# Threshold attention and an exact-GELU MLP on one core: the first batch's x^T by halves, identity matmuls in two kinds of slots, and an MLP share dealt over two slots

## The chip, the cores and the metric

The kernel runs on one core of one Trainium2 chip. The metric is the device time of one launch in microseconds. Two changes in time can be told apart here when they differ by about 0.3%, some 4 us.

## The reference

All of it is float32. q, k and v are (batch 8, heads 8, sequence 576, head dimension 64), tau is a scalar of 0.02. Attention keeps the scores near the maximum of each row:

```
scores = q k^T / sqrt(64)
thresh = rowmax(scores) - tau
scores = where(scores >= thresh, scores, -1e9)
attn   = exp(scores - rowmax);  attn /= sum(attn) + 1e-9
x      = attn v                       # (8, 8, 576, 64)
x      = x transposed to (4608, 512)  # heads side by side
h      = x w_in                       # w_in 512 x 2048
y      = gelu_exact(h) w_out          # w_out 2048 x 512
```

The output y is (4608, 512).

## The kernel before

**Pairs, chunks and slots.** Two heads of one batch are a pair: 32 pairs, of which the first batch has numbers 0 to 3. A pair's 576 query rows are five chunks: four of 128 rows for each head, and one of 64 rows with both heads together. The main loop goes over slots n, one for each pair p and chunk i, in this order: chunks 0 and 1 of pairs 0 to 3 (n = 0 to 7), chunks 2 to 4 of pairs 0 to 3 (n = 8 to 19), and from BATCH = 20 on the five chunks of pair 4, of pair 5, and so on. The weights and the later inputs are still being loaded while the first batch runs.

**A slot.** Everything is written out by hand, in the order in which the engines shall take it; each engine works through its own list in that order.

1. `scores` (L403): TensorE multiplies the chunk with k, two heads at a time, into two PSUM buffers with the tag "sc"; there are two of them, so the next slot's scores wait until this slot has done with its own.
2. `softmax_head`: VectorE takes the row maxima (L415), ScalarE the exponentials (L418), GpSimd the thresholds (L416). Between the thresholds GpSimd adds the low bits of a piece of weights (L226).
3. In the first batch, what is `due`: `weigh_v` multiplies the weights of the pair's finished rows with v to x^T (L538) into a PSUM buffer with the tag "mm", and ScalarE copies it to its place in the token block (L548); `divide_early` spreads the reciprocal sums by matmuls (L457), ScalarE copies them (L459), and GpSimd multiplies x^T by them (L465).
4. `fill` gives TensorE a share of the MLP: matmuls of the first layer (L614) or of the second (L629). How many is a matter of a planner's debt: `owed` is the planned progress in blocks of 256 tokens times the planner's price of a block, and each matmul takes its planner's price off it.
5. `turn_p_early` of the slot before: TensorE transposes the weights (L349) into "mm" buffers and ScalarE copies them to pT (L356, L365), where x^T needs them.
6. `softmax_tail`: VectorE keeps the weights that reach the threshold and sums them (L435); in the first batch the sums go to a small tile with the tag "den", of which there are four.
7. `convert`: ScalarE (L202, L203) and VectorE (L210, L212) turn pieces of w_in and w_out, which came in as raw bits, into float32; GpSimd's addition follows in a later slot.

From slot 20 on `fill` stands at the end of a slot, `turn_p` is a VectorE transpose (L499), and the regrouping is done by DMA.

**Where the first batch's x^T stands.** Rows 0 to 255 of a pair are chunks 0 and 1. Chunk 1 of pair p is computed in slot 2p + 1, turned in the next slot, and put on `due` at the end of that one; so x^T of those 256 rows is made in slot 2p + 3. Slots 4, 6 and 8 come between and have no x^T; of these, slots 6 and 8 have scores and transposes alone (slot 4 has the turning of pair 3's q and k beside them). Rows 256 to 575 follow in the same manner after chunk 4. The first MLP matmul needs the first 256 rows of all four pairs, and is planned for slot 10.

**PSUM.** The tag "mm" has four buffers, which go round in turn: x^T, divisors, transposes and both MLP layers allocate from it.

**Slot 20.** It is the first of the second batch; the held GELUs of the first token block are run there, so `fill` is left out and what is owed goes to slot 21.

**Start.** Before the loop VectorE zeroes `q_tail` and all of the four v tiles (L1028), since parts of a v tile's last chunk stay unwritten.

Of the kernel before, what the change touches and what calls it, by code (L numbers as in the profile page):

```python
# [8 lines left out]
FP32 = mybir.dt.float32  # L9
# [9 lines left out]
def kernel(  # L19
# [28 lines left out]
    nc = tc.nc  # L48
    ctx.enter_context(tc.manual_schedule())

    B, H, S, D = q.shape
    d_model, d_ff = moe_w_in.shape
    P = 128
    Q = 32
    HP = H // 2
    NP = B * HP
    EARLY = HP
    NC = S // P
# [4 lines left out]
    KR = -(-NB // 4)  # L63
    N_DM = d_model // P
    N_DF = d_ff // P
    TOK = 256
# [6 lines left out]
    SLOTS = NC + 1  # L73
# [4 lines left out]
    small = ctx.enter_context(tc.tile_pool(name="small", bufs=4))  # L78
    dram = ctx.enter_context(tc.tile_pool(name="dram", bufs=1, space=bass.MemoryType.DRAM))
    ps = ctx.enter_context(tc.tile_pool(name="ps", bufs=4, space=PSUM))  # L80
# [4 lines left out]
    xall = const.tile([P, XSLOTS, N_DM, TOK], FP32, name="xall")  # L85
# [14 lines left out]
    x_at = {}  # L100

    def x_slot(want=None):
        i = max(x_free) if want is None else want
        x_free.remove(i)
        return i

    def x_place(n):

        last = XSLOTS - 1
        if n >= PLAIN + len(AWAY):  # L110
            return min(x_free)
        return last if n == PLAIN - 1 else max(i for i in x_free if i < last or n < 3)
# [8 lines left out]
    ident = const.tile([P, P], FP32, name="ident")  # L121
# [3 lines left out]
    q_tail = [att.tile([P, P], FP32, name=f"q_tail{i}") for i in range(4)]  # L125
    v_sb = [att.tile([P, 2, KR, D], FP32, name=f"v{i}") for i in range(4)]
# [18 lines left out]
    idle = ps.tile([P, 2 * P], FP32, tag="mm", name="idle")  # L145
# [98 lines left out]
    st = {}  # L244
    x_blk = {}
# [48 lines left out]
    def load_v_early(p):  # L294
        b, hp = divmod(p, HP)
        t = st[p]["v"] = v_sb[p % 4]
        for e in range(2):
            nc.sync.dma_start(t[:, e, 0:NC, :], v[b, 2 * hp + e, 0:MAIN, :].rearrange("(p t) d -> p t d", p=P))
            nc.sync.dma_start(t[e * TAIL:(e + 1) * TAIL, e, NC, :], v[b, 2 * hp + e, MAIN:S, :])

    def turn_qk_early(p):


        s = st[p]
        if 2 <= p < HP:
            qT = op.tile([P, MAIN], FP32, tag="o_sb", name="qT")
            kT = pd_tail[p - 2].rearrange("p b i -> p (b i)")
        else:
            qT = ld.tile([P, MAIN], FP32, tag="qT", name="qT")
            kT = ld.tile([P, TAIL + S], FP32, tag="kT", name="kT")  # L310
        s["qT"], s["kT"] = qT, kT
        qt = s["q_tail"] = q_tail[p % 4]
        copy = nc.scalar.copy if p else nc.vector.tensor_copy
        for name in "qk":
            t = s[name]
            tr = ps.tile([P, NC, P], FP32, tag="mm", name="tr")
            for c in range(NC):
                for e in range(2):
                    nc.tensor.matmul(tr[e * D:(e + 1) * D, c, :], lhsT=t[:, e, c, :], rhs=ident, start=True, stop=True)
            src = tr.rearrange("p c s -> p (c s)")  # L320
            if name == "q":
                nc.scalar.activation(qT, src, AF.Copy, bias=0.0, scale=q_scale)
            else:
                copy(kT[:, TAIL:S], src)
        tr = ps.tile([P, NC, P], FP32, tag="mm", name="tr")
        for j, name in enumerate("qk"):
            t = s.pop(name)
            for e in range(2):
                nc.tensor.matmul(tr[e * D:(e + 1) * D, j, 0:TAIL], lhsT=t[0:TAIL, e, NC, :],
                                 rhs=ident[0:TAIL, 0:TAIL], start=True, stop=True)  # L330
        x_free.extend(s.pop(name + "_slot") for name in "qk" if name + "_slot" in s)
        nc.scalar.copy(kT[:, S:S + TAIL], tr[:, 1, 0:TAIL])
        nc.scalar.copy(kT[D:P, 0:TAIL], tr[D:P, 1, 0:TAIL])
        for e in range(2):
            rows = slice(e * D, (e + 1) * D)
            nc.scalar.activation(
                qt[rows, e * TAIL:(e + 1) * TAIL], tr[rows, 0, 0:TAIL], AF.Copy, bias=0.0, scale=q_scale[rows])
# [84 lines left out]
    def softmax_tail(p, i):  # L422

        s = st[p]
        sc, thr, w = s.pop(("sc", i)), s.pop(("thr", i)), s["p", i]
        n = len(sc)
        if p < EARLY:
            pair = small.tile([P, 2], FP32, tag="den", name="den")
            den = [pair[:, e:e + 1] for e in range(n)]
        else:  # L430
            at = [e * NC + i if i < NC else 2 * NC for e in range(n)]
            den = [sums[p % 2][:, x:x + 1] for x in at]
        for e in range(n):
            row = w[:, e * S:(e + 1) * S].rearrange("p (h s) -> p h s", h=2)
            nc.vector.scalar_tensor_tensor(  # L435
                row, sc[e][:, :, 0:HALF], thr[:, e:e + 1], row, op0=ALU.is_ge, op1=ALU.mult, accum_out=den[e])
        if p < EARLY:
            nc.gpsimd.tensor_scalar(pair[:, 0:n], pair[:, 0:n], 1e-9, None, op0=ALU.add)
            s["sum", i] = pair[:, 0:n]
# [6 lines left out]
    def divide_early(p, lo, hi):  # L446


        s = st[p]
        b, hp = divmod(p, HP)  # L450
        tr = ps.tile([P, 512], FP32, tag="mm", name="tr")
        for i in range(lo // P, -(-hi // P)):
            den = s.pop(("sum", i))
            to = tr[:, i * P - lo:min((i + 1) * P, hi) - lo]
            for e in range(2):
                one_of, cols = (den[:, e:e + 1], ident) if i < NC else (den, ident[:, e * TAIL:(e + 1) * TAIL])
                nc.tensor.matmul(to[e * D:(e + 1) * D, :], lhsT=one_of.to_broadcast([P, D]), rhs=cols, start=True, stop=True)  # L457
        by = dg.tile([P, S], FP32, tag="inv", name="inv")
        nc.scalar.copy(by[:, 0:hi - lo], tr[:, 0:hi - lo])  # L459
        for n, o, at, size in in_blocks(b, lo, hi):  # L460
            x, y = x_blk[n][:, hp, o:o + size], by[:, at - lo:at - lo + size]
            if size == TOK:
                x = x.rearrange("q (p c) -> q c p", c=2)
                y = y.rearrange("q (c p) -> q c p", c=2)
            nc.gpsimd.tensor_tensor(x, x, y, op=ALU.mult)  # L465
# [57 lines left out]
    def weigh_v(p, lo, hi):  # L523


        b, hp = divmod(p, HP)
        s = st[p]
        xT = ps.tile([P, 512], FP32, tag="mm", name="xT")
        for c in range(KR):
            for e in range(2):  # L530
                f = slice(e * D, (e + 1) * D)
                to = xT[f, 0:hi - lo]
                if p < EARLY:
                    rhs = s["pT"][0 if c == NC else e][:, c, lo:hi]
                else:
                    to = to.rearrange("p (g s) -> p g s", s=2 * Q)
                    rhs = by_64(s["pT"][e])[:, lo // (2 * Q):hi // (2 * Q), c, :]
                nc.tensor.matmul(  # L538
                    to, lhsT=s["v"][:, e, c, :], rhs=rhs, start=(c == 0), stop=(c == KR - 1))
        for n, o, at, size in in_blocks(b, lo, hi):  # L540
            if n not in x_blk:
                x_at[n] = x_slot(x_place(n))
                x_blk[n] = xall[:, x_at[n], :, :]
            to, x = x_blk[n][:, hp, o:o + size], xT[:, at - lo:at - lo + size]
            if p < EARLY and size == TOK:
                to = to.rearrange("q (p c) -> q c p", c=2)
                x = x.rearrange("q (c p) -> q c p", c=2)
            nc.scalar.copy(to, x)  # L548

    def in_blocks(b, lo, hi):  # L550
        while lo < hi:
# [86 lines left out]
    def fill(ns, tokens):  # L638

        mlp["debt"] += ns  # L640
        while True:
            if mlp["next"] is None:
                n = mlp["n"]
                if n == PLAIN or (n + 1) * TOK > tokens:
                    break
                mlp["steps"] = block_steps(n)
                mlp["n"] += 1
                mlp["next"] = next(mlp["steps"])
            took, need = mlp["next"]
            if mlp["debt"] <= 0 or need > converted[0]:  # L650
                break
            mlp["debt"] -= took
            mlp["next"] = next(mlp["steps"], None)
# [370 lines left out]
    for _ in range(2):  # L1024
        load_piece(nc.gpsimd)
    load_early(2)
    for t in q_tail + v_sb:
        nc.vector.memset(t, 0.0)  # L1028
    turn_qk_early(0)
    conv["steps"] = conversions()  # L1030
# [10 lines left out]
    BATCH = HP * SLOTS  # L1041
# [15 lines left out]

    PARTS = 1.3, 1.3, 0.2, 1.3, 0.9

    tokens = 0  # L1060
    owed = 0.0
    due = []
    leaving = []
    loads = iter(())
    for n in range(len(slots) + WEIGH + 1):
# [16 lines left out]
            gelus_held()  # L1082
        table()
        for args in due:
            weigh_v(*args)
            divide_early(*args)
        due = []
# [47 lines left out]
        if not early:  # L1135
            lag[0] = 2 if p < NP else 0
            if n != BATCH:
                fill(owed, tokens)
                owed = 0.0
        if last and last[0] < EARLY:  # L1140
            if last[1] == 1:
                due.append((last[0], 0, TOK))
            if last[1] == NC:
                due.append((last[0], TOK, S))
# [44 lines left out]
```

## Time and profile before

| | |
|---|---|
| median of three runs | 1352.2 us (1350.23 to 1354.08) |
| profiled span | 1351.2 us |
| TensorE busy | 1326.1 us (98%) |
| VectorE busy | 1043.9 us (77%) |
| ScalarE busy | 605.6 us (45%) |
| GpSimd busy | 657.2 us (49%) |
| mean granted TensorE clock | 0.989 |
| first batch (slots 0 to 19), by the scores' starts | 9.4 to 134.4 us |

TensorE (PE in the profile, PEld for its weight loads) is busy nearly all the time, but busy time is also time at a low clock: the profile gives the clock that was granted in each stretch beside it. VectorE is DVE, ScalarE is ACT, GpSimd is POOL. L12 is line 12 of the kernel. A group of instructions is told by its line, engine, operation and tiles. A matmul in fp32 stands in the trace as two instructions, a transpose as one.

### The profile page before, as it was taken

To read this page: it belongs to the slowest core of one execution; us is meant where nothing else is said; L and a number is where in the kernel's file an instruction comes from. 1 tells how busy PE (TensorE), PEld (TensorE's weight loads), DVE (VectorE), ACT (ScalarE), POOL (GpSimd) and SP (SyncE) were. 2 spreads that over 40 slices of the span, in tenths; PEclk is the share of its full clock that TensorE was granted. 3 is DMA by queue.
4 is the path that set the end of the run, shared out by engine and by line. 5 is a ranking of instruction groups with operands and counts; after the bars stand their busy time and mean duration, and the time that the engine had idled before them with its cause. 6 is when DMAs were issued, how large, how long until landed. Compare 5 with 4: busy or idle time off the path is not lost.

```text
span 1351.2 us, 19824 instructions
## 1 busy us (share of the span) xinstructions
PE 1326.1 (98%) x6282; PEld 895.3 (66%) x6282; DVE 1043.9 (77%) x2005; ACT 605.6 (45%) x1027; POOL 657.2 (49%) x1091
## 2 busy tenths in 40 slices
PE   8899899999999999999999999999999999999998
PEld 6577457467467467457557557568787787877877
DVE  6877687788888888878888888874758698385775
ACT  7877437438447538437638536413201112211120
POOL 4766444555655565554554551144363513635530
PEclk8899899999999999999999999999999999999999
DMA  8743276677778687787688677500000031000003
GB/s 258 188 137 76 67 168 147 149 169 182 159 179 176 159 202 168 162 207 167 153 210 181 150 180 150 117 8 0 1 0 1 16 110 32 0 1 0 1 0 78
DMA packets 209782, 152.40 MB, mean 113 GB/s; under 512 B 113360, under 2 KB 193088, under 8 KB 209680
## 3 DMA queue, kind: packets, MB, share of 16 engines
q1 hardware_dynamic: 187648, 110.43, 37.1%
q0 software_dynamic: 21312, 39.37, 10.5%
q10 hardware_dynamic: 720, 1.34, 0.3%
q8 instruction: 51, 0.84, 0.3%
q14 instruction: 51, 0.42, 0.1%
HBM read 55.97 MB, written 12.52 MB: 51 GB/s over the span
## 4 chain that ended last, share of the span: by engine, by line
PE 93%; ACT 2%; DMA 2%; DVE 1%; issue 1%; POOL 0%; SPq 0%; DVEq 0%; ACTq 0%; POOLq 0%
PE bank L802 34%; PE o_ps L629 17%; PE hT L614 16%; PE sc L403 14%; PE xT L538 11%; DMA x<-xall 1%; DMA q<-in_q_dram 1%; ACT p L418 1%; PE tr L349 1%; DVE nmx L415 1%; ACT pT L356 0%; DVE p L435 0%; PE tr L457 0%; ACT power L202 0%; DVE power L212 0%
## 5 line engine op out<-in xcount | busy, mean ns | idle before, releaser
L418 ACT ACTIVATE p<-sc,nmx 128x576 f32<-128x576 f32 x288 | 201.9, 739 | 278.7 <-DVE nmx L415 278.5
L435 DVE SCALAR_TENSOR_TENSOR p<-sc,thr,p 128x576 f32<-128x576 f32 x288 | 226.2, 816 | 77.9 <-ACT p L418 71.4
L416 POOL TENSOR_SCALAR thr<-nmx,tau_eff 128x1 f32<-128x1 f32 x288 | 85.3, 296 | 369.0 <-DVE nmx L415 359.4
L415 DVE TENSOR_REDUCE nmx<-sc 128x1 f32<-128x576 f32 x288 | 205.4, 750 | 53.4 <-PE sc L403 52.1
L614 PE MATMUL hT<-xall,w_in 128*128 128x256 f32 x1024 | 243.0, 387 | 0.0
L629 PE MATMUL o_ps<-w_out,g 128*128 128x512 f32 x512 | 238.4, 606 | 0.0
L614 PEld LDWEIGHTS hT<-xall,w_in 128*128 128x128 f32 x1024 | 190.4, 191 | 50.5 <-issue 23.0
L684 DVE TENSOR_TENSOR c<-c,bank 128x320 f32<-128x320 f32 x304 | 147.2, 488 | 33.7 <-PE bank L802 20.5
L684 DVE TENSOR_TENSOR o<-o,bank 128x256 f32<-128x256 f32 x240 | 99.8, 420 | 93.7 <-PE bank L802 88.7
L403 PE MATMUL sc<-kT,qT 64*128 64x288 f32 x960 | 161.8, 434 | 9.8 <-DVE p L435 9.1
L538 PE MATMUL xT<-pT,v 128*64 128x256 f32 (+1 forms) x1280 | 168.0, 416 | 0.1
L629 PEld LDWEIGHTS o_ps<-w_out,g 128*128 128x128 f32 x512 | 93.7, 191 | 110.2 <-issue 107.6
L499 DVE STREAM_TRANSPOSE turned_p<-p 128x1152 f32<-128x1152 f32 x112 | 154.4, 1378 | 3.9
L403 PEld LDWEIGHTS sc<-kT,qT 64*128 64x128 f32 x960 | 92.2, 188 | 83.4 <-issue 69.5
L538 PEld LDWEIGHTS xT<-pT,v 128*64 128x64 f32 x1280 | 91.4, 140 | 75.3 <-issue 14.6
L802 PE MATMUL bank<-w_out,c 128*128 128x256 f32 x480 | 120.2, 381 | 0.5 <-DVE o L684 0.5
L269 POOL DMA_DIRECT2D v<-in_v_dram x208 | 111.3, 538 | 3.7 <-issue 1.3
L802 PEld LDWEIGHTS bank<-w_out,c 128*128 128x128 f32 x480 | 89.9, 190 | 18.8 <-DVE o L684 3.0
L855 ACT ACTIVATE c<-c 128x320 f32<-128x320 f32 (+1 forms) x80 | 46.9, 623 | 114.6 <-DVE c L684 114.5
L684 POOL TENSOR_TENSOR c<-c,g 128x320 f32<-128x320 f32 (+1 forms) x40 | 50.6, 1273 | 67.4 <-DVE c L684 67.4
L802 PE MATMUL bank<-t_out,c 128*128 128x256 f32 x320 | 82.7, 381 | 0.0
L802 PE MATMUL bank<-t_out,g 128*128 128x256 f32 x320 | 82.1, 379 | 0.0
(179 smaller groups left out, 1771.8 us busy)
## 6 DMA issues: line engine op xcount, KB each, us to landing
pT<-turned_p SPq DMA_DIRECT2D x448, 160.0 KB, 3.6
pT<-pd_tail SPq DMA_DIRECT2D x112, 80.0 KB, 3.0
q<-in_q_dram POOLq DMA_DIRECT2D x104, 72.0 KB, 3.8
k<-in_k_dram POOLq DMA_DIRECT2D x104, 72.0 KB, 3.2
inv<-turned SPq DMA_DIRECT2D x54, 128.0 KB, 4.0
v<-in_v_dram POOLq DMA_DIRECT2D x156, 40.0 KB, 3.1
out_dram<-o SPq DMA_DIRECT2D x40, 128.0 KB, 2.4
xall<-in_moe_w_out_dram POOLq DMA_DIRECT2D x9, 512.0 KB, 4.4
```

The costliest lines, as they stand in the source:

```text
L269: eng.dma_start(t[r:P:4, e, 0:n, :], rows[:, r * KR:r * KR + n, :])
L403: nc.tensor.matmul(sc[e][:, h, 0:HALF], lhsT=lhsT, rhs=s["kT"][rows, at:at + HALF], start=True, stop=True)
L415: nc.vector.tensor_reduce(nmx[:, e:e + 1], sc, axis=AXIS.XY, op=ALU.max, negate=True)
L416: nc.gpsimd.tensor_scalar(thr[:, e:e + 1], nmx[:, e:e + 1], -1.0, tau_eff, op0=ALU.mult, op1=ALU.subtract)
L418: nc.scalar.activation(w[:, e * S:(e + 1) * S].rearrange("p (h s) -> p h s", h=2), sc, AF.Exp, bias=nmx[:, e:e + 1], scale=1.0)
L435: nc.vector.scalar_tensor_tensor(row, sc[e][:, :, 0:HALF], thr[:, e:e + 1], row, op0=ALU.is_ge, op1=ALU.mult, accum_out=den[e])
L499: nc.vector.transpose(turned_p[:, :, i // 2, 0:NB, i % 2 * Q:(i % 2 + 1) * Q], w.rearrange("p (e b i) -> p e b i", e=2, i=Q))
L538: nc.tensor.matmul(to, lhsT=s["v"][:, e, c, :], rhs=rhs, start=(c == 0), stop=(c == KR - 1))
L614: nc.tensor.matmul(hT[:, j % 2, :], lhsT=w_in_sb[c][:, j * P:(j + 1) * P], rhs=x_blk[n][:, c, :], start=(c == 0), stop=(c == N_DM - 1))
L629: nc.tensor.matmul(o[:, 0:d_model], lhsT=g[j][:, m * P:(m + 1) * P], rhs=w_out_sb[j], start=(j == 0), stop=(j == N_DF - 1))
L684: eng.tensor_tensor(out, a, b, op=ALU.add)
L802: nc.tensor.matmul(to, lhsT=l, rhs=r, start=start and k == 0, stop=k == len(pairs) - 1, skip_group_check=not start)
```

## The change

All of it concerns the first batch and the two slots after it.

- `weigh_half` makes x^T of one chunk, 128 rows, of pairs 2 and 3 as soon as that chunk is turned: chunk 0 in slots 6 and 8, chunk 1 (with the division of both) in slots 7 and 9.
- `keep_busy` multiplies the identity with itself into an "mm" buffer that nobody reads: four fp32 matmuls at the end of slots 6 and 8, eight at the end of slot 20. It is there to hold TensorE's clock up where it would otherwise have nothing to do.
- What is owed to the MLP at slot 21 is dealt out as 0.4 of it in slot 21, and the rest in slot 22.
- The tag "den" has ten buffers instead of four.
- Of the v tiles only the last chunk is zeroed at the start.

```diff
+    def keep_busy(times):
+        idle = ps.tile([P, 2 * P], FP32, tag="mm", name="idle")
+        for _ in range(times):
+            for c in range(2):
+                nc.tensor.matmul(idle[:, c * P:(c + 1) * P], lhsT=ident, rhs=ident, start=True, stop=True)
...
-            pair = small.tile([P, 2], FP32, tag="den", name="den")
+            pair = small.tile([P, 2], FP32, tag="den", name="den", bufs=2 * SLOTS)
...
+    def weigh_half(p, c):
+        hp = p % HP
+        s = st[p]
+        if 0 not in x_blk:
+            x_at[0] = x_slot(x_place(0))
+            x_blk[0] = xall[:, x_at[0], :, :]
+        xT = ps.tile([P, 512], FP32, tag="mm", name="xT")
+        cols = slice(c * P, (c + 1) * P)
+        for k in range(KR):
+            for e in range(2):
+                nc.tensor.matmul(xT[e * D:(e + 1) * D, 0:P], lhsT=s["v"][:, e, k, :],
+                                 rhs=s["pT"][0 if k == NC else e][:, k, cols], start=(k == 0), stop=(k == KR - 1))
+        nc.scalar.copy(x_blk[0][:, hp, :].rearrange("q (p c) -> q c p", c=2)[:, c, :], xT[:, 0:P])
...
-    for t in q_tail + v_sb:
+    for t in q_tail + [t[:, :, NC, :] for t in v_sb]:
         nc.vector.memset(t, 0.0)
...
+    HALVED = (2, 3)
+    BUSY = {6: 2, 8: 2, BATCH: 4}
...
         for args in due:
+            if len(args) == 2:
+                weigh_half(*args)
+                if args[1]:
+                    divide_early(args[0], 0, TOK)
+                continue
             weigh_v(*args)
             divide_early(*args)
...
             if n != BATCH:
-                fill(owed, tokens)
-                owed = 0.0
+                share = 0.4 if n == BATCH + 1 else 1.0
+                fill(owed * share, tokens)
+                owed *= 1.0 - share
+        if n in BUSY:
+            keep_busy(BUSY[n])
         if last and last[0] < EARLY:
-            if last[1] == 1:
+            if last[1] < 2 and last[0] in HALVED:
+                due.append((last[0], last[1]))
+            elif last[1] == 1:
                 due.append((last[0], 0, TOK))
```

## The prediction

> **What bounds the kernel now.** I read the page's 40 slices first: where is TensorE not busy, and where is its clock below full?
>
> ```profile
> PE   8899899999999999999999999999999999999998
> ...
> PEclk8899899999999999999999999999999999999999
> ```
>
> Only slices 0, 1 and 4 (33.8 us each) have a clock digit of 8. Busy time by stage (columns: us of the stage, busy us and instructions of PE, PEld, DVE, ACT and POOL, granted clock, DMA share, GB/s) says the same:
>
> ```profile
> 10.00:170.00 160.00, 145.21 (x870) 98.32 (x869) 117.49 (x236) 115.04 (x229) 97.84 (x161) 0.92 0.51 141
> 165.00:1351.20 1186.20, 1178.80 (x5379) 793.65 (x5378) 925.11 (x1759) 488.62 (x793) 558.37 (x925) 1.00 0.48 108
> ```
>
> After 165 us TensorE is busy 99.4% at clock 1.00: nothing in the change shortens that, and whatever time is won before it should move the end one for one, since its fills, loads and softmaxes are written out in a fixed order. Before it 14.8 us are idle and the clock is 0.92.
>
> Next the TensorE timeline of the first batch, for gaps. A bracket gives the idle time before and its releaser; "xN" are instructions, and an fp32 matmul is two of them.
>
> ```profile
> 43.44 1.20 PE L349 MATMUL tr<-ident,p 128*128 128x128 f32 x9
> 47.41 3.42 PE L403 MATMUL sc<-pd_tail,qT 64*128 64x288 f32 x8 [2.77 <-DVE p L435]
> 50.77 4.06 PE L538 MATMUL xT<-pT,v 128*64 128x256 f32 x20
> ...
> 61.14 3.01 PE L403 MATMUL sc<-kT,qT 64*128 64x288 f32 x8 [2.44 <-DVE p L435]
> 64.08 4.23 PE L538 MATMUL xT<-pT,v 128*64 128x256 f32 x20
> ...
> 138.24 0.72 PE L403 MATMUL sc<-kT,qT 64*128 64x288 f32 x2 [1.94 <-DVE p L435]
> ...
> 158.20 1.94 PE L403 MATMUL sc<-kT,qT 64*128 64x288 f32 x8 [1.58 <-DVE p L435]
> 160.07 6.21 PE L629 MATMUL o_ps<-w_out,g 128*128 128x512 f32 x10
> ```
>
> These are slots 7, 9, 21 and 23. Each gap is in a slot with scores and transposes alone, and after each the same instructions run long: eight score matmuls take 1.24 us elsewhere (at 42.27), the twenty of x^T 2.65 (at 37.91), ten of the second layer 4.56 (at 171.03). Cut into stretches of 3.41 us the clock is seen to switch whole stretches:
>
> ```profile
> 43.76:47.18 3.42, 0.88 (x9) 0.64 (x6) 3.24 (x6) 3.24 (x6) 1.96 (x3) 1.00 0.83 226
> 47.18:50.59 3.41, 3.18 (x8) 1.70 (x8) 3.00 (x8) 3.19 (x7) 2.75 (x6) 0.53 0.25 96
> 50.59:54.00 3.41, 3.41 (x17) 1.91 (x18) 2.93 (x7) 1.41 (x2) 2.57 (x5) 0.50 0.90 252
> ...
> 57.41:60.83 3.42, 1.29 (x11) 0.97 (x9) 2.50 (x5) 3.42 (x7) 2.68 (x5) 1.00 0.72 256
> 60.83:64.24 3.41, 3.10 (x10) 1.97 (x12) 3.38 (x9) 3.23 (x7) 2.75 (x4) 0.53 0.13 50
> ...
> 77.89:81.30 3.41, 2.46 (x14) 1.67 (x14) 2.93 (x8) 3.19 (x8) 3.06 (x4) 1.00 0.18 73
> ...
> 135.92:139.33 3.41, 1.09 (x6) 0.43 (x4) 2.92 (x8) 2.89 (x4) 2.77 (x4) 1.00 0.00 0
> 139.33:142.74 3.41, 3.37 (x12) 1.82 (x14) 3.33 (x7) 3.40 (x7) 1.02 (x7) 0.53 0.02 5
> ...
> 156.40:159.81 3.41, 1.81 (x9) 1.00 (x8) 3.16 (x6) 1.39 (x2) 2.67 (x6) 1.00 0.42 94
> 159.81:163.22 3.41, 3.41 (x6) 1.50 (x5) 3.37 (x7) 0.56 (x1) 0.91 (x2) 0.53 0.27 65
> ```
>
> A stretch with 0.88, 1.29, 1.09 or 1.81 us of matmuls is followed by one at half clock; one with 2.46 is not. So the line lies somewhere between 53% and 72% busy.
>
> **What the skill says.** "TensorE: Matmul & The Clock Gate", Part 1, says that the clock is either half or full and is judged over a free-running window of 3413 ns; the stretches above agree (0.50 to 0.53 or 1.00, edges a multiple of 3.41 us apart). Its "HAM oscillation" section asks for no idle gap above some 3.4 us; the trace is stricter: a gap of 1.58 us sufficed, and the trace decides. The section on the array's architecture says that ScalarE and VectorE are strict FIFOs; the trace agrees (the copy of x^T at 54.90 stands behind both exponentials of its slot), and it matters below.
>
> **The change, part by part.** First site, slots 6 to 9. The gap before 47.41 ends with VectorE's threshold product of slot 6, so filling it does not shorten slot 6; it may keep the clock up in slot 7. There the work was 3.42 + 4.06 + 0.44 (divisors) + 1.13 (transposes), about 8.9 us. With half of x^T gone to slot 6 and full clock it is 1.17 + 1.45 + 0.45 + 1.13 = 4.2. Halves cost what wholes do: twenty instructions of 64 weight columns by 128 at 70 ns, taken between the 66 ns of L319 (16 in about 1.05 us) and the 75 ns of L457 (8 in 0.60): 1.4 us, against 2.65 for 256 columns. Two halves are thus dearer by 0.15 us, in slack.
>
> TensorE then no longer sets slots 7 to 9; ScalarE does. Its chain, copied from the trace: it starts slot 6's conversions at 48.00. A new copy of a half x^T (0.28, as the 128-column L365) stands before, so 48.3. Exponentials of slot 7 follow at 51.87 (before 51.59), 1.41; half x^T 0.28; divisors 0.37; pT copies up to the next conversion 1.25: 55.2, against 57.06 (it sat idle 1.91 before 54.90 for x^T). Slot 8: conversions 2.25, exponentials 1.24, the second new copy 0.28, pT 1.1: 60.1, against 61.66. Slot 9: VectorE's maxima are held by these conversions, so the exponentials start at 63.2 (64.77 less 1.6), then 1.41, 0.28, 0.37, 1.25: 66.5, against 70.54. Slot 10's scores may start when slot 9's first product frees their bank, 66.61 - 1.6 = 65.0, and end at 66.0. But the first MLP matmul needs pair 3's division on GpSimd, which stands behind two weight additions: 67.98 - 1.6 + 0.8 = 67.2. So L614 starts at 67.3 instead of 70.85: **3.5 us**. From there to slot 20 TensorE has only seven gaps with 2.7 us in all, so this is carried.
>
> The identity matmuls: slots 6 and 8 get 4 (8 instructions), slot 20 gets 8 (16). The trace has no 128x128 fp32 matmul with 128 weight columns; L349's transposes run at 107 to 126 ns (9 in 1.13), the L614 rate halved gives 108, and at half clock it would be double. I take 120: 0.95 us and 1.9 us; the ends are 0.85 and 1.9 for the former. They add a wait: the "mm" buffers go round four at a time (at 35.84 the second transposed group waits for qT's copy, four allocations back). In slots 6 and 8 the allocations are x^T, three for transposes, then idle: so idle waits for the copy of x^T, which stands behind the exponentials, to 47.3 and 59.0. Queued behind it are the next scores, free at 47.6 and about 59.4: they start at 48.3 and 60.0, 0.6 to 0.7 late. Who waits for the scores is VectorE's maxima, which have conversions before them up to 51.1 and 62.3. Hidden. In slot 20 idle has a buffer copied at 135.0 and ends 136.30 + 1.9 = 138.2, just when the scores start anyway.
>
> Second site, slots 20 to 24. Full clock at 139.33: x^T starts at 141.0 (its pT copy on VectorE at 140.56 comes first), takes 2.84, ends 143.85 instead of 145.06: 1.2 us. The owed share of both slots is 2 x 1.42/24 x 54,613 x 1.3 = 8,402 in the planner's ns; at 853 each that made ten L629 matmuls in slot 21 (x20), one in slot 22. With 0.4 of it slot 21 gets four, slot 22 seven (5,041 + 646 - 52). Slot 22's scores move from 154.32 to 143.85 + 0.55 + 4 x 0.88 = 147.9; their bank is free at 147.1, since the exponentials of slot 21, held by gelus and two table loads, still start at 145.30. While seven matmuls run, 149.1 to 155.2, VectorE does slot 22 and finishes its first product near 151.6. So slot 23 starts at 155.2 without a gap, 3.0 earlier; at full clock its scores save 0.75 and its ten instructions 6.14 - 4.45 = 1.7. Slot 24 starts at 160.7: **5.4 us** in all. No matmul is added but the identities.
>
> The deeper den ring removes a wait of the products of slots 12, 15, 18 for the divisors; the trace shows one of 0.9 us, under twelve to fourteen L614 instructions: nothing. V's memset falls from 2.61 us to about 0.7, but the first scores also wait for a ScalarE copy of the tail (9.22): at most 0.03 us. Sum 3.5 + 5.4 = 8.9; 1352.2 - 8.9 = 1343.3.
>
> **Rivals.** (a) The first site gives nothing: a stretch of the new slots 6 to 9 still falls below the line (in slot 8 TensorE would be idle 57.6 to 59.0), half clock stays, and the divisions come as late as now. For it: ACT at 4.96 of slot 6's 5.14 us, and the waiting identities. Against: 1.2 to 1.4 us idle in 3.41 is milder than any stretch that tripped. Then 1352.2 - 5.4 = 1346.8. (b) Sites give half: the stretches fall otherwise, or slot 22 waits for data: gain 2 to 4, 1349.5. (c) Slower: the identities hold up the scores and the clock still drops, so they run doubled: scores then start 1.6, 1.5 and 1.9 us late in slots 7, 9 and 21 (47.3 + 1.9 against 47.6, and so on), of which the conversions hide some 2, and no stretch is won: 1352.2 + 3 = 1355. Against: what the identities fill is idle now, so the stretch is busier than before. (d) More: GpSimd's division does not hold L614, slot 10 starts at 65.0 as the bank allows, and a later gap closes: gain 11, 1341.
>
> **How the numbers follow.** Forecast 0.52, (a) 0.18, (b) 0.12, (c) 0.07, (d) 0.11. The bound of 0.3% is 4.1 us. Forecast and (d) are faster, nearly all of (a) too: 0.78; (b) and the rest of (a) within: 0.14; slower 0.08. Range 1339.5 (below (d), with spare for the clock's phase) to 1349.8 (past (a) and most of (b)); it leaves out (c) and a little beside.
>
> **What would show it.** Right: half clock gone after 47, 60, 139 and 156 us; slot 10's L614 near 67.3; L629 x8 then x14 in slots 21 and 22, no gap before slot 23's scores; PE's slice 4 digit of the clock at 9; from 170 us the same rows, some 9 us earlier. Wrong: half clock in those stretches, scores of slots 7 or 9 held so that the maxima start later, or a new gap after slot 24 that gives time back.

## The result and the profile after

The changed kernel takes 1339.7 us (median of five runs, 1337.4 to 1340.7) where the kernel before takes 1352.2. The ratio is 0.9905, with a 95% interval of 0.9891 to 0.9919, so the change brings 12.8 us. Measured a second time it was 0.9923 (0.9907 to 0.9938), 10.4 us. The forecast was a gain of 8.9.

The 40 slices of the changed kernel's page show the digit of the clock at 9 in slices 0, 1 and 4, where it was 8. Slice 0 is no part of the gain: half clock near 10 and 20 us comes and goes from trace to trace of one kernel, and two of the four traces of the changed kernel have a stretch of it near 20 us.

```profile
PE   8899999999999999999999999999999999999998
...
PEclk9999999999999999999999999999999999999999
```

Busy time by stage in the changed kernel (columns as in the prediction: stage, its us, busy us and instructions of PE, PEld, DVE, ACT, POOL, granted clock, DMA share, GB/s):

```profile
10.00:160.00 150.00, 139.95 (x942) 97.44 (x941) 119.24 (x236) 114.69 (x231) 99.00 (x162) 1.00 0.55 151
160.00:1338.60 1178.60, 1172.46 (x5365) 790.02 (x5361) 921.22 (x1753) 486.96 (x791) 552.80 (x918) 1.00 0.46 108
```

The first 160 us of this trace are at full clock. That says the half-clock stretches went, not yet how much each was worth. For this the TensorE timeline of the changed kernel at both sites (start us, us, engine, line, operation, tiles, count, and in brackets the idle time before with its releaser):

```profile
40.58 1.24 PE L410 MATMUL sc<-pd_tail,qT 64*128 64x288 f32 x8
...
45.53 1.16 PE L306 MATMUL idle<-ident 128*128 128x128 f32 x8 [1.33 <-ACT xall L571]
46.62 1.42 PE L410 MATMUL sc<-pd_tail,qT 64*128 64x288 f32 x8
47.97 1.31 PE L569 MATMUL xT<-pT,v 128*64 128x128 f32 x20
...
57.20 1.16 PE L306 MATMUL idle<-ident 128*128 128x128 f32 x8 [0.80 <-ACT xall L571]
58.29 1.87 PE L410 MATMUL sc<-kT,qT 64*128 64x288 f32 x8
...
64.71 1.46 PE L637 MATMUL hT<-xall,w_in 128*128 128x256 f32 x6
66.33 1.99 PE L637 MATMUL hT<-xall,w_in 128*128 128x256 f32 x8 [0.16 <-POOL xall L472]
...
130.62 1.95 PE L306 MATMUL idle<-ident 128*128 128x128 f32 x16
...
135.58 3.14 PE L545 MATMUL xT<-pT,v 128*64 128x320 f32 x20 [0.52 <-DVE pT L367]
...
139.20 3.70 PE L652 MATMUL o_ps<-w_out,g 128*128 128x512 f32 x8
142.83 1.24 PE L410 MATMUL sc<-kT,qT 64*128 64x288 f32 x8
144.00 6.28 PE L652 MATMUL o_ps<-w_out,g 128*128 128x512 f32 x14
150.21 1.24 PE L410 MATMUL sc<-kT,qT 64*128 64x288 f32 x8
151.38 4.56 PE L652 MATMUL o_ps<-w_out,g 128*128 128x512 f32 x10
```

This is the picture that the forecast drew: the identities stand behind the copies of x^T (brackets of 1.33 and 0.80 us), the second layer is dealt as 8 and 14 instructions, and slot 23's scores at 150.21 follow without a gap. Yet the gain is larger. To find the rest, the span is cut by the starts of the scores of slots 6, 11, 20, 24, 105 and 155. One pair of traces doesn't do: two more were taken of each kernel beside the repeats, so that each mean is over four.

| stretch, us | before, mean of 4 (range) | after, mean of 4 (range) | difference |
|---|---|---|---|
| start to slot 6 | 42.1 (41.4 to 43.0) | 41.5 (40.6 to 42.9) | -0.6 |
| slot 6 to 11 (first site) | 31.8 (30.3 to 32.8) | 28.7 (28.6 to 28.7) | -3.1 |
| slot 11 to 20 | 59.6 | 59.6 | 0.0 |
| slot 20 to 24 (second site) | 31.8 (31.7 to 31.8) | 26.9 (26.9 to 27.0) | -4.8 |
| slot 24 to 105 | 413.7 | 413.7 | 0.0 |
| slot 105 to 155 | 257.2 (256.6 to 258.5) | 253.9 (252.8 to 254.4) | **-3.4** |
| slot 155 to the end | 514.7 | 514.7 | 0.0 |

The sum, 11.9, is the difference of the mean spans (1351.0 and 1339.0). Some 8 us come from the two sites, where 8.9 were forecast; the 0.6 of the first row lie within its ranges. Another 3.4 come between 570 and 830 us, where no line was changed. In the kernel before, something happens there at slot 109. Its timeline across the engines (SPq is SyncE issuing a transfer; `x<-xall` is the put-away of a finished token block to memory, of which two are issued here):

```profile
592.02 0.54 SPq L667 DMA_DIRECT2D x<-xall  x1
...
593.08 1.05 SPq L667 DMA_DIRECT2D x<-xall  x1
...
597.92 0.43 ACT L548 COPY xall<-xT 128x128 f32<-128x128 f32 x2 [3.92 <-DMA x<-xall]
...
601.22 0.27 ACT L548 COPY xall<-xT 128x128 f32<-128x128 f32 x1 [2.86 <-DMA x<-xall]
601.38 1.38 ACT L418 ACTIVATE p<-sc,nmx 128x576 f32<-128x576 f32 x2
602.23 0.82 DVE L435 SCALAR_TENSOR_TENSOR p<-sc,thr,p 128x576 f32<-128x576 f32 x1 [3.18 <-ACT p L418]
...
603.21 1.73 PE L403 MATMUL sc<-kT,q_tail 128*128 128x288 f32 x4 [1.96 <-DVE p L435]
```

Read it from the end. TensorE stood idle for 1.96 us before slot 109's scores, which waited for VectorE's product; this waited for the exponentials; these stood in ScalarE's queue behind a copy of x^T; and the copy waited 2.86 us until the place in `xall` that it overwrites had been put away. The copies before it had waited 3.92 us for the first put-away; the last one waits for the second. The maxima that the exponentials need were ready at 599.05, so ScalarE does take its list in order here; the prediction read this from the copy at 54.90, which merely waited for its own data. The four score instructions take 1.73 us instead of 1.13: half clock. The stage view of the kernel before has both, the idle time and the clock, in one line:

```profile
600.00:610.00 10.00, 8.04 (x31) 5.79 (x30) 5.78 (x13) 5.59 (x8) 5.71 (x11) 0.83 0.80 182
```

The same chain in the changed kernel, the same view:

```profile
581.45 0.54 SPq L690 DMA_DIRECT2D x<-xall  x1
...
582.51 0.88 SPq L690 DMA_DIRECT2D x<-xall  x1
...
586.09 0.43 ACT L555 COPY xall<-xT 128x128 f32<-128x128 f32 x2 [2.44 <-DMA x<-xall]
...
589.76 0.27 ACT L555 COPY xall<-xT 128x128 f32<-128x128 f32 x1 [3.24 <-DMA x<-xall]
...
591.74 1.21 PE L410 MATMUL sc<-kT,q_tail 128*128 128x288 f32 x4 [0.86 <-DVE p L442]
```

From the second put-away's issue to the copy that it lets go are 7.25 us instead of 8.14 (for the first it is 4.64 instead of 5.90); the gap is 0.86 instead of 1.96 us, and the clock stays. It is the second that sets the gap: in every trace with SyncE's put-aways and such a gap, the scores of slot 109 start 2.0 us after the start of that copy. In this pair of traces the stretch differs by 2.2 us only (256.6 and 254.4). By the means of the four, the gap is 2.3 us before and 0.7 after, a difference of 1.6, and a stretch of 3.41 us at half clock costs another 1.7: together 3.3 of the 3.4 us.

### The profile page after: what moved, and what is told of

It is laid out like the page before. It is cut to its first block, busy times and chain, and to the rows that moved or that the text cites. A ratio compares the mean times of both kernels' runs of the same rounds, so it can differ in the third digit from the quotient of the medians.

```text
span 1338.6 us, 19954 instructions
## 1 busy us (share of the span) xinstructions
PE 1320.5 (99%) x6354; PEld 893.9 (67%) x6354; DVE 1043.3 (78%) x2005; ACT 604.9 (45%) x1029; POOL 656.0 (49%) x1091
## 4 chain that ended last, share of the span: by engine, by line
PE 93%; DVE 2%; DMA 1%; ACT 1%; POOL 1%; issue 1%; SPq 0%; DVEq 0%; POOLq 0%; ACTq 0%
PE bank L825 34%; PE o_ps L652 17%; PE hT L637 16%; PE sc L410 13%; PE xT L545 12%; DMA q<-in_q_dram 1%; DVE power L212 1%; DMA v<-in_v_dram 1%; POOL w_in L226 1%; DVE nmx L422 0%; PE tr L356 0%; ACT p L425 0%; DVE power L210 0%; ACT pT L363 0%; PE tr L464 0%
## 5 line engine op out<-in xcount | busy, mean ns | idle before, releaser
L410 PE MATMUL sc<-kT,qT 64*128 64x288 f32 x960 | 161.3, 429 | 2.6 <-DVE p L442 2.6
L545 PE MATMUL xT<-pT,v 128*64 128x320 f32 (+1 forms) x1240 | 159.6, 409 | 0.7 <-DVE pT L367 0.5
L545 PEld LDWEIGHTS xT<-pT,v 128*64 128x64 f32 x1240 | 86.5, 137 | 71.5 <-issue 10.8
```

Of the source, the lines that this page charges most:

```text
L410: nc.tensor.matmul(sc[e][:, h, 0:HALF], lhsT=lhsT, rhs=s["kT"][rows, at:at + HALF], start=True, stop=True)
L545: nc.tensor.matmul(to, lhsT=s["v"][:, e, c, :], rhs=rhs, start=(c == 0), stop=(c == KR - 1))
```

## The experiments

The theory after the result: two clock sites as forecast, and a third, unforeseen one at slot 109. Its rivals: that the zeroing of V, the deeper "den" ring or a later start accounts for the rest; that the clock is kept by the halves alone or the identities alone; and that the difference at slot 109 is chance. Unless said otherwise the ratio is to the kernel before on the same chip, with its 95% interval.

**The kernel before against itself.** No edit. It shows what no change looks like.

> The kernel before, once more, for a second trace of it. Both theories: ratio 1.000. Theory 1 (half clock near 12 and 21 us and the wait for a put-away transfer near 600 us belong to the kernel): they are seen again, at the same instructions. Theory 2 (they are chance, since the clock's windows fall anew in every run): one or more of them is missing here, and the gaps in slots 7, 9, 21 and 23 may trip the clock at other instructions.

1351.6 us, ratio 0.9993 (0.9984 to 1.0002). Its stretch from slot 105 to 155 was 256.8 us.

**V's last chunk alone**

```diff
-    for t in q_tail + v_sb:
+    for t in q_tail + [t[:, :, NC, :] for t in v_sb]:
```

> The kernel before with one line of the change: of the v tiles only the last chunk is zeroed. Theory 1 (the memset held the copy of kT, and the first score matmul needs only that copy, not the tail's): the first scores start about 0.7 us earlier than in before, slot 3's scores 1 to 2 us earlier, and the end moves by 0.7 to 1.7 us (ratio 0.9987 to 0.9995). Theory 2 (the early start seen with the whole change was the clock's phase or a transfer's chance): start and end as in before, ratio 1.000.

1350.7 us, 0.9988 (0.9977 to 0.9999): some 3 us at most. Slot 105 to 155 took 257.6 us, slots 6 to 11 33.0, as before. The smaller zeroing does not bring the late gain.

**The first site alone.** The halves, and identities in slots 6 and 8:

```diff
+    HALVED = (2, 3)
+    BUSY = {6: 2, 8: 2}
```

> The kernel before with x^T by halves for pairs 2 and 3 and the identities of slots 6 and 8 alone. Theory 1 (sites are independent and add): 3.9 us faster, as slots 6 to 10 gained in the whole change, ratio 0.9971. Theory 2 (the gain of these slots leaned on the early start, since the clock's windows fell well): 2 us or less.

1346.9 us, 0.9966 (0.9954 to 0.9979), 4.6 us by the ratio. By stretches: 28.6 us for slots 6 to 11 (as in the whole change), 31.9 for slots 20 to 24 (as before), 254.7 for slots 105 to 155.

**The second site alone.** The share of 0.4, and identities in slot 20:

```diff
+    HALVED = ()
+    BUSY = {BATCH: 4}
...
+                share = 0.4 if n == BATCH + 1 else 1.0
```

> The kernel before with the share dealt over slots 21 and 22 and the identities of slot 20 alone. Theory 1 (sites add): 4.9 us faster, ratio 0.9964. Theory 2 (the late 2.1 us, near 600 us, come with this site, which shifts the loads): 7 us faster, ratio 0.9948, and no half-clock stretch near 600 us.

1347.1 us, 0.9963 (0.9949 to 0.9976), 5.0 us. Slots 6 to 11 31.6, slots 20 to 24 26.9, slots 105 to 155 254.3. The two sites are independent of each other, but either one also makes the late stretch some 2.5 to 3 us shorter. The late gain is thus not a sum, and no single edit is its cause. Nor does it take a changed first batch: this kernel's is the old one.

**Identities away, the rest of the change kept**

```diff
-    BUSY = {6: 2, 8: 2, BATCH: 4}
+    BUSY = {}
```

> The changed kernel without any identity matmul; halves, shares, den and memset stay. Theory 1 (the identities carry the clock): slots 7, 9 and 21 run partly at half clock again, each costing what TensorE then holds up; slot 21 about 1.2 us, slots 7 and 9 up to 2 us together: 1 to 3 us slower than the changed kernel, that is ratio 0.9913 to 0.9928 to before. Theory 2 (the halves alone fill slots 6 and 8 enough, and identities only hold the scores up by 0.9 us each): 0.9905 or below.

1342.2 us, 0.9933 (0.9919 to 0.9947). Its TensorE timeline:

```profile
46.67 2.25 PE L410 MATMUL sc<-pd_tail,qT 64*128 64x288 f32 x6 [0.45 <-DVE p L442]
48.86 2.40 PE L569 MATMUL xT<-pT,v 128*64 128x128 f32 x20
...
135.75 4.30 PE L545 MATMUL xT<-pT,v 128*64 128x320 f32 x20 [0.37 <-DVE pT L367]
```

Half clock is back in slot 7 (the half x^T takes 2.40 instead of 1.31) and in slot 21 (4.30 instead of 3.14). Yet slots 6 to 11 took 29.0 us, only 0.4 more than with identities, and slots 20 to 24 28.1, 1.2 more. Keeping the clock up is worth little where the other engines set the pace.

**Halves away, identities kept**

```diff
-    HALVED = (2, 3)
+    HALVED = ()
```

> The changed kernel with whole x^T for pairs 2 and 3 again; the identities of slots 6, 8 and 20 and all else stay. Theory 1 (the clock is what counts at the first site, and identities alone hold it): slots 7 and 9 then run 1.2 us longer each on TensorE than with halves, ScalarE's chain hides most of it, and the kernel is at most 1 us slower than the changed one: ratio 0.9905 to 0.9913. Theory 2 (the halves are the gain: 1.0 us of identities in a 2.7 us gap do not hold the clock): 3 us slower, 0.9928.

1342.4 us, 0.9935 (0.9916 to 0.9955), not to be told from the whole change, which gave 0.9923 (0.9907 to 0.9938) beside it. The median is 1.4 us above that one's, between the two theories, and the trace has its extra time in the late stretch (255.6 us against a mean of 253.9), not at the first site. The timeline of slots 7 and 9:

```profile
47.48 4.07 PE L545 MATMUL xT<-pT,v 128*64 128x256 f32 x20
...
59.83 2.38 PE L545 MATMUL xT<-pT,v 128*64 128x256 f32 x20
```

Slot 7 is still cold, slot 9 is warm, and slots 6 to 11 took 28.9 us, 0.2 more than the whole change. At the first site the halves or the identities alone give nearly all; both together are hardly better.

**V zeroed whole, the rest kept**

```diff
-    for t in q_tail + [t[:, :, NC, :] for t in v_sb]:
+    for t in q_tail + v_sb:
```

> The changed kernel with all of the v tiles zeroed at the start as before. Theory 1 (the memset holds kT's copy and with it the first scores): scores of slot 0 at 9.4 to 10.5 us instead of 8.0 to 8.8, and 1.2 to 1.6 us slower at the end, ratio 0.9914 to 0.9917. Theory 2 (the first tail of q lands too late to let it count): 0.9905.

1341.0 us, 0.9924 (0.9910 to 0.9939), the same as the whole change. Over all traces, slot 0's scores start at about 9.7 us with whole tiles zeroed and 8.6 with the last chunk, so the edit does move the first scores by about 1.1 us; but slot 6 starts anywhere from 40.1 to 44.4 us in the one kind and from 40.0 to 43.9 in the other.

**Identities without a buffer of their own.** They are written to unused columns of the last transposed tile, so that they need not wait for a buffer:

```diff
-        idle = ps.tile([P, 2 * P], FP32, tag="mm", name="idle")
...
-                nc.tensor.matmul(idle[:, c * P:(c + 1) * P], lhsT=ident, rhs=ident, start=True, stop=True)
+                nc.tensor.matmul(spare[0][:, 1 + c, :], lhsT=ident, rhs=ident, start=True, stop=True)
```

> The changed kernel with the identities written into unused columns of the slot's last transpose tile, so that they allocate no buffer and do not wait for the copy of x^T. Theory 1 (the wait is hidden, since VectorE has conversions before its maxima): the scores of slots 7 and 9 start 0.6 to 0.9 us earlier, but slot 10 and the end do not move by more than 0.3 us: ratio 0.9905. Theory 2 (the wait costs): 1 to 1.8 us faster, 0.9892 to 0.9898.

1347.8 us, 0.9972 (0.9963 to 0.9981): 7 us slower than the whole change, which neither theory expected. The timeline of slot 20:

```profile
137.29 3.78 PE L307 MATMUL tr<-ident 128*128 128x128 f32 x16 [5.51 <-DVE pT L377]
141.00 2.29 PE L411 MATMUL sc<-kT,qT 64*128 64x288 f32 x8
```

The identities now wait 5.51 us until that tile has been read to pT, slot 21's scores stand in the queue behind them, and the gap that the identities should fill becomes longer. Slots 20 to 24 took 33.3 us, more than in the kernel before.

**Put-aways issued by GpSimd instead of SyncE.** If the put-away's wait is the late site, moving its issue out of SyncE's queue should show there. Done to the kernel before, and to the changed one:

```diff
-        nc.sync.dma_start(away[n], x_blk.pop(n))
+        nc.gpsimd.dma_start(away[n], x_blk.pop(n))
```

> The kernel before with that same queue for the put-aways and nothing else. Theory 1: the gap of 2.0 to 2.2 us near 600 us and the half-clock stretch after it go, 3 us faster, ratio 0.9978, so that the change's parts are compared on equal ground. Theory 2: 0.9995 or above.

The kernel before with this one edit: 1347.8 us, 0.9980 (0.9971 to 0.9989), nearly 3 us faster. Slots 105 to 155 took 253.6 us instead of 257.2; the two sites are as before (32.4 and 31.8). The edit changes when the put-aways are issued: counted from the scores of slot 105, at 3.3 and 11.9 us instead of 12.2 to 12.6 and 13.2 to 13.7, since in SyncE's queue they stand behind the four transfers of the divisors. The second then lands 4.5 us after its issue instead of 7.9 to 8.5, and neither the gap before slot 109 nor the half clock is there. So the wait for a put-away is what costs the kernel before these 3.6 us.

> The changed kernel with the five put-away transfers of token blocks issued by GpSimd's queue, not behind the divisors' transfers in SyncE's. Theory 1 (of the whole change's gain 2 us arose near 600 us, where a put-away landed 1.2 to 2 us sooner and the gap in TensorE stayed below what trips the clock): here only the remaining gap of 0.9 us is left to win, ratio 0.9898 to 0.9902. Theory 2 (that wait is hidden elsewhere): 0.9905 or, if GpSimd's issues cost it, above.

The changed kernel with it: 1340.6 us, 0.9913 (0.9898 to 0.9927). Slots 105 to 155 took 251.7 us, 2.2 less than the mean of the changed kernel. Its timeline at slot 109:

```profile
581.28 0.57 POOL L690 DMA_DIRECT2D x<-xall  x1
...
586.40 0.27 ACT L555 COPY xall<-xT 128x128 f32<-128x128 f32 x1 [0.71 <-DMA x<-xall]
...
590.64 1.13 PE L410 MATMUL sc<-kT,q_tail 128*128 128x288 f32 x4
```

The wait for the second put-away is 0.71 us and TensorE has no gap. With the put-aways moved in both kernels, the ratios 0.9913 and 0.9980 leave some 9 us (1352 x 0.0067; 7 to 11 with both intervals) for the change itself, near the 8.9 that were forecast. That the two sites alone make it up is not shown: the late stretch still differs by 1.9 us between these two traces (253.6 and 251.7). The kernel before has a new gap there, 0.80 us in slot 110, where VectorE waited 2.30 us for a threshold of GpSimd's; a second trace of it was not taken.

**Both once more, side by side.** The changed kernel, and the changed kernel with GpSimd's put-aways, without further edit.

> The changed kernel once more, beside the next run. Both theories: ratio 0.9905 to before. Theory 1 (near 600 us the put-away's landing differs from run to run, and the gain there is partly luck): the gap before the scores near 592 us lies between 0.3 and 2 us, and half clock may follow. Theory 2 (the changed kernel lands them sooner always): 0.9 us and full clock again.

> The changed kernel with the put-aways in GpSimd's queue, once more. Theory 1 (put-aways cost the kernel before 3 us and the changed one 1 us, since its gaps no longer trip the clock): 1 us faster than after_again, ratio 0.9898 to before. Theory 2 (they cost both alike): 3 us faster, 0.9883. If neither: no difference, 0.9905.

0.9923 (0.9907 to 0.9938) against 0.9902 (0.9884 to 0.9920). Over ten runs each the medians are 1340.6 and 1338.3 us. Both traces with GpSimd's put-aways show 251.7 us for the late stretch, 2.2 less than the mean of the changed kernel, but the timed intervals overlap: it has the lowest median seen, and the times alone do not settle it.

The second trace of it shows something else. Its identities ran in slots 6, 8 and 20 as always, yet slots 8 and 21 are partly at half clock. In slot 21:

```profile
138.94 4.78 PE L545 MATMUL xT<-pT,v 128*64 128x320 f32 x20 [0.52 <-DVE pT L367]
```

Slots 20 to 24 took 28.6 us there instead of 26.9. Of the nine traces with eight identity matmuls in slot 20 this is the only one with half clock in slot 21: the identities keep the clock up nearly always, not always.

**Is the late difference chance?** Two more traces of each kernel, no edit.

> The kernel before, for a third trace. Theory 1 (the wider gap near 600 us belongs to the kernel before): a gap of 1.9 us or more before the scores of slot 109 with the clock halved after it, as in the three traces of it and of the memset alone. Theory 2 (chance): a gap of 0.4 to 1.8 us as in the changed family in at least one of the two repeats. Start: slot 5's scores anywhere from 34.4 to 38.7 us.

> The kernel before, for a fourth trace. Theory 1: a gap of 1.9 us or more at slot 109 and half clock after it. Theory 2: 0.4 to 1.8 us here or in the third.

> The changed kernel, for a third trace. Theory 1: the gap at slot 109 is below 1.9 us and the clock stays full. Theory 2: it is 2 us or more here or in the next one. Start: slot 5's scores anywhere from 34.4 to 38.7 us.

> The changed kernel, for a fourth trace. Theory 1: the gap at slot 109 is below 1.9 us and the clock stays full. Theory 2: 2 us or more here or in the third.

They took 1353.4, 1351.5, 1340.6 and 1340.0 us. From the second put-away's issue to its copy took 8.5 and 8.4 us in the kernel before, with gaps of 2.58 and 2.54; 7.1 and 6.3 us after, with gaps of 1.44 and none. The ranges of the four traces each (gaps of 1.96 to 2.58, and of 0 to 1.44) do not meet, so this is hardly chance.

**Time of launch or program?** The first put-away falls at 590 to 592 us before and at 581 to 585 after. One theory (the first in these expectations) is that what else the DMA engines do at that moment decides; the other, that the order of the program does. 52 identities in slot 20 shift the changed kernel to about where the old one stood; the same shift takes the old one further.

```diff
-    BUSY = {6: 2, 8: 2, BATCH: 4}
+    BUSY = {6: 2, 8: 2, BATCH: 26}
```

> The changed kernel with 52 identity matmuls in slot 20 instead of 8: all that follows comes some 10 us later, so that the put-aways of slot 106 and 107 are issued at 591 to 593 us, when the kernel before issues them, and not at 581 to 583. Theory 1 (something at a fixed time of the launch slows transfers near 592 to 597 us, and the changed kernel has passed that place by then): the first put-away is copied over 5.7 us or more after its issue, and the gap before slot 109's scores is 1.9 us or more. Theory 2 (the program itself, not the hour, makes it land sooner): 4.0 to 5.2 us and a gap below 1.8 us, as in the changed family.

> The kernel before with 52 identity matmuls in slot 20: all that follows comes some 9 us later, put-aways at 600 to 602 us. Theory 1 (a fixed time of the launch): the first put-away lands within 5.2 us and the gap is below 1.8 us. Theory 2 (the program itself): 5.7 us or more, and a gap of 1.9 us or more, as in the four traces of the kernel before.

There is one run of each. The shifted changed kernel took 1348.7 us, its put-aways fell at 589.5 and 591.9, their copies came 5.1 and 5.6 later, and slots 105 to 155 took 254.7: still the shorter time. The shifted old kernel (first batch as before, identities in slot 20 alone) took 1360.2, and 257.4 for that stretch. Its timeline:

```profile
599.22 0.54 SPq L690 DMA_DIRECT2D x<-xall  x1
...
600.29 0.93 SPq L690 DMA_DIRECT2D x<-xall  x1
...
603.45 0.43 ACT L555 COPY xall<-xT 128x128 f32<-128x128 f32 x2 [3.09 <-DMA x<-xall]
...
607.52 0.27 ACT L555 COPY xall<-xT 128x128 f32<-128x128 f32 x1 [3.64 <-DMA x<-xall]
...
609.51 1.76 PE L410 MATMUL sc<-kT,q_tail 128*128 128x288 f32 x4 [1.90 <-DVE p L442]
```

Here both transfers are as quick as in the changed kernel (4.23 and 7.23 us from issue to copy), as the time of launch would have it; the gap of 1.90 us and the half clock stay, because the put-aways were issued 0.4 to 0.9 us later in the slots than in the kernel before. But the shifted changed kernel's second put-away fell within the old one's hours (591.4 to 593.4) and took 5.6 us instead of 7.9 to 8.5, as the program would have it, though it was issued 2.4 us behind the first and not 1.1. Neither theory holds alone, and the question stays open.

## Why the prediction was right or wrong

The forecast was 1343.3 us and the result 1339.7. The gain was put too low by some 3 us (8.9 against 11.9 by the mean spans). The two sites brought 7.9, a little less than forecast; what was missing lies in one step.

- **The step that failed** is "nothing in the change shortens that, and whatever time is won before it should move the end one for one", said of the time after 165 us. Its term was 0; it measured 3.4 us, from slot 105 to 155. TensorE was indeed busy 99.4% there at a mean clock that reads 1.00, but 0.6% of 1186 us is 7 us, and one of these gaps tipped the clock. The wait of a copy for a put-away stood in the old trace, and no term of the prediction has it. What is shown: moving the put-aways' issue alone takes 3.6 us out of the old kernel's stretch (257.2 to 253.6), so this wait is what costs it. What is not shown is why the second put-away lands sooner (6.1 to 7.2 us after its issue instead of 7.9 to 8.5) when both sites, or either alone, are changed.
- **The line for the clock**, "somewhere between 53% and 72% busy", was read from one trace and does not hold over the others: a stretch with 2.37 of 3.41 us busy (69%) was followed by half clock (at 53.8 us in the second trace of the changed kernel with GpSimd's put-aways), one with 1.60 (47%) was not (at 45.2 us with the second site alone). What decides is open.
- **First site: right in mechanism, a little large in size.** Forecast 3.5, measured 3.1 by the means. In the two profiled traces themselves it is 32.5 to 28.6; the old kernel varies by 2.5 us with where the half-clock stretches fall, the changed one by 0.04. With the start of slot 6 put equal (1.69 us added to the after times), the idles start at 47.2 and 58.9 (forecast 47.3 and 59.0), slot 7's and 9's scores at 48.3 and 60.0 (the same), the scores of slot 10 at 65.4 (65.0). The conversions hid the late scores, as worked out. One detail was wrong: the first MLP matmul came at 66.4, not 67.3, since six instructions use pairs 0 to 2 only and go before pair 3's division. The division itself ended later than worked out, at 68.0 instead of 67.2, but the seventh instruction waits just 0.16 us. The identities there, which the forecast let share in the work, are worth 0.4 us beside the halves.
- **Second site: right in mechanism, a little large in size.** Forecast 5.4, measured 4.8. With slot 20 put equal (5.51 us added), x^T starts at 141.1 (forecast 141.0), slot 22 at 148.3 (147.9), slot 23 at 155.7 (155.2), slot 24 at 161.3 (160.7); each is a little late. About 1.2 of the 4.8 us come from the identities, the rest from the share of 0.4.
- **Identities' price:** 8 in 1.06 to 1.16 us and 16 in 1.95; forecast 0.95 and 1.9. **The halves' price:** 1.31 us for twenty, against 1.4.
- **The "den" ring at nothing: right.** Slots 11 to 20 take 59.6 us with four buffers and with ten.
- **V's zeroing: wrong about the start, the end not to be told.** The first scores move by about 1.1 us, since they do not wait for the tail copy that was named (in the profiled trace they start at 8.76 us, that copy at 8.88); with whole tiles or the last chunk alone the changed kernel took the same time (0.9924 and 0.9923), and the start of slot 6 scatters by 4 us.
- **The rivals.** (a) and (b) fell with the first site, (c) with the clock at 1.00. (d) came nearest in its number, and that is luck: the division did not hold the first MLP instructions, but only because they do not need it, and that was worth about 0.9 us at most, not 2; the remainder is the late stretch, which no rival held.

## What to carry to other kernels

Where a busy share of 99% is to mean "nothing to win here", list the gaps that make up the last per cent with their releasers: one gap of 2 us that tips the clock costs a half-clock stretch besides, here 1.7 us. Work out what a slot's slowest engine allows before pricing a clock that is kept up: half clock in slot 7 cost 0.2 to 0.4 us at most here, where ScalarE's conversions set the pace. A matmul that is only there to keep the array busy needs an output that no reader holds, or it waits itself and everything behind it in the queue.

## What the runs showed of the hardware

- A TensorE gap of 1.96 us at slot 109 was enough for half clock in the stretch that followed, and one of 0.86 us was not. In the six traces where this gap was longest (the four of the kernel before, V's zeroing alone, and the shifted kernel before; 1.90 to 2.96 us) half clock followed; in the eleven others with SyncE's put-aways it was 1.77 us or less, with full clock. The Trainium skill ("TensorE: Matmul & The Clock Gate", section "HAM oscillation") asks for gaps below some 3.4 us; these traces show less to be too much. Length alone does not decide: the 1.58 us before slot 23 were followed by half clock in every trace that has them, the 1.77 at slot 109, in the changed kernel with V zeroed whole, were not.
- With SyncE issuing, the time from a first put-away's issue to the copy that it lets go lay between 4.0 and 6.9 us, and differed by kernel more than from one trace to the next of a kernel: 5.8 to 6.2 us in four traces before, 4.3 to 4.6 in four after. For the second, issued 1.1 us behind in these eight, it was 7.9 to 8.5 and 6.3 to 7.3.
- The start of slot 6 varies from 40.0 to 44.4 us from trace to trace, over kernels with the same or nearly the same start. A single pair of traces can therefore be wrong by 4 us in the first batch alone, as much as each site is worth.
